# A planned attention and squared-ReLU kernel: the first batch's P.V split instead of zeroed, the first weights in two loads, and one Strassen block of tokens made plain again

## The chip, the cores and the metric

The kernel runs on one core of a Trainium2 chip. The metric is the device time of one execution in microseconds. Before the change the median of three runs is 288.12 us. The engines are TensorE (PE; its weight loads are shown apart as PEld), VectorE (DVE), ScalarE (ACT), GpSimd (POOL) and SyncE (SP).

## The reference

Eight batches of eight heads, 576 positions of head size 64. Attention within a window of 32 positions to each side, then a two-layer network with squared ReLU over all 4608 tokens:

```python
scores = q @ k^T / sqrt(64)                       # per batch and head, 576 x 576
scores = where(|i - j| <= 32, scores, -1e9)
attn = exp(scores - max) / (sum + 1e-9)
x = (attn @ v)  -> [4608 tokens, 512]             # heads side by side
h = x @ w_in                                      # 512 -> 2048
out = (max(h, 0) ** 2) @ w_out                    # 2048 -> 512, float32
```

## The kernel before

**Attention.** Each batch is three parts of 192 query positions, 24 parts in all, numbered G = 0 to 23. For a part, k and q are loaded as bf16 (`load_qk` on POOL's queue, L377; three of the first loads go through `load_hw` on SP and ACT as float32 into `ts` and are cast, L391 to L394). Parts below NTG = 9 are transposed on PE (`turn_pe`, L463) and copied to `kq` by ACT or DVE (L476, L477); the others by a transposing DMA (`turn_dma`, L491). `scores` multiplies keys by queries for two blocks of 128 keys (w = 0 and 1), eight heads each (L531), takes exp on ACT (L554), and multiplies by the 0/1 mask on DVE (L562): with MP = 1 both blocks in one instruction, unless the part is below NSPLIT = 6.

`pv` multiplies the probabilities by v with a column of ones (L590), twice into the same pair of banks: after the first (w = 0), rows 64 to 127 of the bank are finished; they are divided by their sums (L604, L608) into `xa`. After the second, all 128 rows are finished and divided into `xb`. Between them, rows 64 to 127 are set to zero (L614 on ACT or L615 on DVE), since the second product adds to what stands there. For parts below NZ there is no zeroing: the second product of each head is made in two column halves of its weights, and the half for rows 64 to 127 starts afresh:

```python
split = w and not full                     # full = G >= NZ
for z in range(0, 128, 64 if split else 128):
    n = 64 if split else 128
    mm = e.matmul(ps[z:z + n, c:c + 65], ptt[:, 4 * (h % 2) + h // 2, z:z + n], vt[:, w, h, 0:65],
                  start=((w == 0 or (z == 64 and split)) and y == 0), stop=True, skip_group_check=True)
```

`xturn` transposes x, on PE for parts below NXT = 9 (L630, L636, copied to `xt` by L644 or L646, called XT), later by DMA on SP.

**Network.** Tokens go through w_in in tiles of 192, 192, 192, 192 and 256, then 512. `mm1` (L690) is the plain form: 16 blocks of 128 hidden units, each four matmuls as wide as the tile, then ReLU (L664, L665) and square (L659, L660). For a tile in PAIR two blocks share a two-bank tile and one ReLU of 1024 columns. `mm1s` (L770) is the Strassen-Winograd form of a 512-token block: for each of four groups of hidden units seven products of four 256-column matmuls, with sums on DVE (L742, L794, L800) and seeds and copies on ACT (L809, L670). It is used for the blocks that MM1S lists. The second layer is plain for the first four tiles of 128 tokens (`mm2`, L835) and seven products for each later block (`strassen`, L917, with its sums on DVE, L859, L885, L949). A `wash` (L895) is one matmul of zeros over a bank, where the order's list of slots marks it with w.

Weights come on POOL's queue: w_in in four column quarters (`load_w1`, L431), w_out in four row quarters (`load_w2`, L436). With W1H a quarter of w_in comes in two loads.

**Order.** Every operation is recorded once, with its reads and writes. A text, ORDER, gives each recorded operation a letter for its engine (P, A, D, G for POOL, S for SP) and a start in nanoseconds; it is followed by the slot of each buffer. `apply` sorts each engine's instructions by these starts; nothing else is taken from them at run time, and semaphores hold the order between engines. Before 40 us `fill` puts small matmuls on zeros (L299) into the planned gaps of PE, at one for 56 ns, and ahead of the first transposes 39 plus one for every 56 ns beyond 3.9 us.

Of the kernel before, what the change touches and what calls it, by code (L numbers as in the profile page):

```python
# [21 lines left out]
    MM1S=(2048, 2560, 3072, 3584, 4096),  # L22
# [9 lines left out]
    PAIR=(1536,),  # L32
# [6 lines left out]
    W1H=(),  # L39
    TAIL=0,  # L40
    FP=1,
    MP=1,
    S34=1,
    NZ=0,
# [5 lines left out]
    NPT=4,  # L50
# [182 lines left out]
class Gen:  # L233
# [7 lines left out]
    def alloc(self):  # L241
# [733 lines left out]
    def record(self):  # L975
# [81 lines left out]
        at(4.0, self.sums_w2, 4.0)  # L1057
        if cfg["MM1S"]:
            at(4.5, self.sums_w1, 4.5)
# [30 lines left out]
P12475 D13910 D14180 D14966 P15634 D16146 D16416 P15114 P17172 A17612 P10615 D11167 P11225 A12456 P13361 A13996 D15461  # L1090
P13786 A15024 D18507 P16216 D17102 D17822 A18577 P19276 D19746 D20016 P19536 P20851 D21291 P15344 A16867 P14211 A16052
P17665 A19186 D21843 P20426 A21061 D24619 P22598 D23081 D23933 A25450 P26388 D27094 D27364 P24838 P28702 D30325 G20932
G21768 G20096 G16920 G24920 G29504 P41968 D42573 P40496 A41308 P43262 A43897 D45015 P18517 D22528 P43687 A45477 D46595
P19766 A23151 A24140 P45774 D46386 D47280 D48036 P49140 D49610 D49880 P51114 P51344 D51838 P21081 A23646 P23518 D25304
A27788 P26648 A28603 P27308 A29188 D29773 P29592 D34242 G23392 G22604 G27188 G27976 G43361 G45917 P45432 D48531 P47354
A47906 P28042 D34864 A35487 P49400 A50035 D51153 P24178 D25856 P51574 A52352 D53470 P25068 A26479 A29683 P52442 D53127
D54155 D54911 P55806 D56291 D57177 P57386 P58583 D59595 P21913 D23281 D33556 D38025 D37340 D38711 D35969 D45700 D43192
D57862 P22858 A24955 A26974 P25728 D30878 D26409 D32871 D28050 D36654 D28735 D40069 D31430 D32185 P30912 A32202 A32787
P30252 A31122 G26448 G28764 G24180 G25708 G46801 G48521 P47696 D49083 P47986 A49216 P28932 A31707 A36301 P50689 A51324
D52442 P31572 D35417 P51999 A53380 D55406 P44772 A47399 A57337 P55546 D56091 D56491 D58548 P59473 D60148 D60900 P58011  # L1100
P62644 D63084 P36348 D40754 P46034 A46904 A55037 P33960 D39396 P34620 P37008 P38736 P40891 A42229 A59141 P42363 A43233
D50565 P44112 A44982 G45081 G44245 G52653 G47685 G59793 G63781 P57616 A59521 P59733 A60443 P46694 A48721 D64189 P61994
A62994 A64112 D65507 P52702 A55852 P54886 A56842 A62179 P67289 D67759 D68029 A68941 P73039 D73509 D73969 P74079 P75183
A75994 P33096 P35484 P37872 P39632 A40706 A94765 P56066 A58646 P58813 D60348 A61364 P54226 A56347 P56726 A58152 D75340
P60992 D63636 G51029 G42573 G55017 G54229 G58121 G50145 P58241 D59043 P61652 D62204 P32232 P48276 P49825 P53362 A54436
S113850 P76293 A78955 A80051 P65775 A66795 A67913 D69031 P68422 A69549 P71033 D71620 D71890 D72645 P73299 D73769
D74655 P73849 P75413 D75893 P67549 A70240 D70934 P63738 D64821 P64611 A65695 D70249 P60128 P62874 P66425 P69295 A70842
A129316 P71293 A72376 G67125 G57381 G53489 G55805 G65453 G59005 P73559 A74059 P65485 D66725 P74309 A75393 D77130
G56545 G51817 G62945 G49309 G64665 G87303 P75643 A76809 A77927 D79045 S69616 S68326 P70159 A71443 P81919 D82389 D82659
A83760 P84769 D85318 D85588 P103901 P105644 D106314 P72166 A73249 D76445 P77816 A79450 D80263 D86274 D83345 D88177  # L1110
D84100 P85893 P86767 A87851 P89154 P94023 D99960 D95953 A104236 P90288 P91162 D92246 P97154 P98891 A99975 P94897
P102153 D104943 S139197 P101279 P103027 D106866 A116182 P105874 P106748 A107832 A121814 P79543 D80948 A81704 P82179
A85997 P85029 A86689 A95145 G61369 G66337 G60581 G62157 G79875 G75935 P81269 A82732 A84368 D86959 S67036 S71616 P76953
D78026 P90028 D93131 D93401 A94157 P96634 D99005 D99275 S94157 S100030 P83906 A85396 D88863 P80406 D81634 P83043
D89548 A96173 P78679 A80866 P98028 D101178 D101934 G77607 G68701 G69441 G78347 G86419 G104247 P87641 A88501 A89619
D90737 S83639 S91003 P92296 D96638 P92036 D92931 D94087 D95458 P96894 D97364 D97634 S102530 S101280 P95771 A97394
D98319 P88291 A90647 P93159 D94772 D105628 P99765 A103635 P104781 A107159 D108769 G75099 G80759 G84699 G67865 G76819
G100393 P100629 A101489 A102607 D103725 S95407 S92293 P115980 P117103 A118177 A122194 D102619 D116722 D111687 D117608
D112915 P114232 P115106 A116562 P118227 P119101 D120503 A120185 S128302 P121098 P124573 D125657 P122835 P126960
A130126 P127834 P128708 D132956 S140937 P133035 P135657 D136741 S137497 P133909 P134783 A135867 A145085 P108272  # L1120
D109455 D109725 A110480 P111985 D112455 D114133 S112600 S123182 P119975 P121972 D123292 D124580 P112505 P113369
A114442 D121921 G79087 G83911 G83123 G82335 G85535 G107255 P104131 A105013 A106131 D107551 S88423 S96697 P110259
P111122 A112195 A120786 P112245 D112715 D114819 A115574 P117967 D118437 D119322 S115574 S120642 P131309 P132172
A133245 A134363 P108532 P109395 D110469 D131165 G74359 G105775 G81595 G106515 G113703 G108975 P107622 A108839 A111088
D115504 S89713 S111310 P123709 P125447 D128729 D134746 P116843 D117408 D118637 D120008 P120838 D121721 D122606 S119392
S137947 P129582 P130445 A131519 D134060 D132536 D133641 D126840 D135431 P136531 A137178 P138055 D138702 A140576
P138492 D139388 P139820 A141177 P140517 D141869 P142702 D143772 A148131 D155834 P143399 A145465 A150362 P137618
A139974 P140954 A143077 D154996 P142265 A143678 P143836 A144483 P145147 D145794 P145584 D146691 D148062 D149699
P146718 A147530 A151565 P146281 A146928 P148029 A149159 A155866 P150651 D151298 P151348 A152167 P152222 D152939
P153096 D154310 D155415 A156467 P153970 A155264 A160153 P148466 A149761 P151785 A152768 A153460 P152659 D153625  # L1130
P153533 A154663 P155281 D156557 P158116 D159103 D162111 D164054 P159427 A160754 A161446 D128044 D131851 D135851
D140073 D137427 P138946 P141391 A142475 P144273 P147155 D148482 A150964 S154259 P148903 P149777 A154061 P154407
P155718 A158523 P157242 P158553 D159788 S160544 P159864 P161388 D163369 S164124 P162262 P163136 A164220 S190571
G109763 G110599 G90491 G108139 G111435 G134127 P126310 A127170 A128288 D129947 S124432 S125722 P140257 D140759 D141029
A141784 P143139 D144458 D144728 S146733 S145483 G116259 G117047 G117835 G99605 G133243 G140625 P136968 A137828 A138946
D142554 S130042 S128752 P146021 D146491 D147377 D150385 P151088 D151984 D152254 S150563 S153009 G112223 G112963
G105035 G103507 G160271 G141509 P156592 A157495 A159125 D160474 S127012 S121892 P164447 D164917 D165187 A166025
P167766 D168462 D169359 S165943 S185090 D158684 D161692 D162950 D162530 P164010 A164822 P165581 A166633 D180492
P166018 D167091 P167329 A167976 P168026 D168673 P168900 D170044 D172948 A175430 P169774 A170421 A173626 P164707
A165423 P166455 A168578 D176379 P166892 A169781 P169337 A172334 P170648 D173367 P174664 D175693 A177060 D182129  # L1140
P174227 A176458 D187961 P165144 A167234 P168463 A169179 A174829 P170211 A171023 P171085 A171732 P171782 D176798
P176849 D178169 D180073 A181534 P184751 A185398 A186601 P179684 A180331 P181869 A182562 A188976 P182566 A183213
# [80 lines left out]
```

## Time and profile before

| | |
|---|---|
| median of three runs | 288.12 us (288.11 to 289.0) |
| the profiled execution's own time | 288.54 us |
| its span, first to last instruction | 286.7 us |
| granted TensorE clock, mean | 1.000 |
| busy: PE, PEld, DVE, ACT, POOL | 280.1, 232.0, 236.0, 201.7, 117.9 us |
| mean DMA rate | 135 GB/s |

The span is shorter than the execution's own time by what lies around the first and last instruction. Busy times are sums of the instructions' spans; a matmul's span overlaps the next, so a busy TensorE is not one at its peak. In a row of the groups stand line, engine, operation, output and input, then busy time and the mean of one, then the idle time ahead of it and what ended it. In the chain of waits each row is a start, a length, and the work on the chain, the last column its number of instructions.

### The profile page before, as it was taken

How to read it: one execution, taken by the hardware profiler on the slowest of the kernel's cores; microseconds unless marked ns; L12 is line 12 of the kernel's file. 1: busy time of each engine (PE TensorE's matmuls, PEld its weight loads, DVE VectorE, ACT ScalarE, POOL GpSimd, SP SyncE). 2: the span in 40 equal slices, each digit the busy share in tenths (PEclk: the TensorE clock that was granted, in tenths of full speed). 3: DMA queues.
4: the chain of work that ended last, by engine and by line, in shares of the span. 5: the costliest groups of instructions: out<-in, count | busy, mean ns of one | idle time of the engine just before them, and what ended most of it. 6: DMA issues, size and time to landing. Idle time of an engine off the chain costs nothing.

```text
span 286.7 us, 7639 instructions
## 1 busy us (share of the span) xinstructions
PE 280.1 (98%) x3097; PEld 232.0 (81%) x3115; DVE 236.0 (82%) x424; ACT 201.7 (70%) x302; POOL 117.9 (41%) x153
## 2 busy tenths in 40 slices
PE   8999999999999999999999999999999999999995
PEld 8979858787857775776898898988888888888884
DVE  2779968878898988979889889899999989979631
ACT  1777638887795476636878899888887768776520
POOL 8999109998693269403702994310000000000000
PEclk9999999999999999999999999999999999999999
DMA  9999999999999999999999999998720431102123
GB/s 147 157 192 204 205 161 148 144 158 148 162 141 150 182 148 143 194 163 186 135 195 158 144 162 155 134 189 137 148 53 13 134 87 40 37 2 71 41 91 130
DMA packets 171107, 38.62 MB, mean 135 GB/s; under 512 B 158272, under 2 KB 170560, under 8 KB 171072
## 3 DMA queue, kind: packets, MB, share of 16 engines
q0 software_dynamic: 121920, 18.98, 94.4%
q1 hardware_dynamic: 43344, 14.30, 29.0%
q10 hardware_dynamic: 5808, 4.85, 5.5%
q8 instruction: 25, 0.41, 0.6%
q14 instruction: 10, 0.08, 0.1%
HBM read 38.80 MB, written 9.44 MB: 168 GB/s over the span
## 4 chain that ended last, share of the span: by engine, by line
PE 93%; DVE 3%; ACT 2%; issue 1%; ACTq 0%
PE ps L917 34%; PE ps L770 22%; PE ps L690 19%; PE ps L835 5%; PE ps L590 4%; PE ps L531 4%; PE ps L299 3%; PE ps L463 2%; ACT e L554 1%; PE ps L630 1%; DVE pt L562 1%; PE ps L636 1%; DVE xa L608 0%; ACT oe L670 0%; DVE xb L608 0%
## 5 line engine op out<-in xcount | busy, mean ns | idle before, releaser
L690 PE MATMUL ps<-xt,w 128*128 128x192 bf16 (+2 forms) x438 | 60.9, 286 | 0.7 <-issue 0.3
L670 ACT ACTIVATE oe<-ps 128x512 f32<-128x512 f32 x62 | 36.0, 596 | 29.4 <-PE ps L917 16.6
L554 ACT ACTIVATE e<-ps 128x1024 bf16<-128x1024 f32 x48 | 48.6, 1021 | 11.0 <-PE ps L531 8.9
L665 ACT ACTIVATE rt<-ps 128x512 bf16<-128x512 f32 (+2 forms) x76 | 44.0, 594 | 16.7 <-PE ps L690 9.6
L377 POOL DMA_DIRECT2D raw<-in_k_dram x46 | 36.4, 810 | 35.9 <-DMA kq<-raw 21.7
L690 PEld LDWEIGHTS ps<-xt,w 128*128 128x128 bf16 x448 | 38.7, 98 | 13.8 <-DVE xt L646 0.3
L377 POOL DMA_DIRECT2D raw<-in_q_dram x46 | 36.9, 815 | 27.3 <-DMA kq<-raw 26.5
L917 PE MATMUL ps<-w,gt 128*128 128x256 bf16 x384 | 47.3, 273 | 0.0
L659 ACT ACTIVATE gt<-rt 128x512 bf16<-128x512 bf16 (+2 forms) x56 | 43.2, 793 | 2.6 <-DVE rt L664 1.8
L415 POOL DMA_DIRECT2D v<-in_v_dram x48 | 42.0, 887 | 6.1 <-PE ps L590 6.1
L917 PEld LDWEIGHTS ps<-w,gt 128*128 128x128 bf16 x384 | 36.8, 98 | 6.0 <-issue 0.6
L562 DVE TENSOR_TENSOR pt<-e,mask 128x2048 bf16<-128x2048 bf16 (+1 forms) x30 | 30.3, 1009 | 3.9 <-ACT e L554 3.5
L770 PE MATMUL ps<-xs,sw 128*128 128x256 bf16 x240 | 32.7, 272 | 0.0
L917 PE MATMUL ps<-ts,gt 128*128 128x256 bf16 x256 | 31.7, 273 | 0.0
L917 PE MATMUL ps<-ts,ss 128*128 128x256 bf16 x256 | 31.4, 273 | 0.0
L794 DVE TENSOR_TENSOR rt<-ps,oe 128x512 bf16<-128x512 f32 x40 | 27.3, 687 | 4.0 <-PE ps L770 3.2
L917 PEld LDWEIGHTS ps<-ts,ss 128*128 128x128 bf16 x256 | 24.4, 98 | 3.7
L917 PEld LDWEIGHTS ps<-ts,gt 128*128 128x128 bf16 x256 | 24.7, 98 | 3.1
L770 PEld LDWEIGHTS ps<-xs,sw 128*128 128x128 bf16 x240 | 23.0, 98 | 2.6
L660 DVE TENSOR_TENSOR gt<-rt 128x1024 bf16<-128x1024 bf16 (+2 forms) x40 | 23.3, 590 | 0.5 <-ACT rt L665 0.4
L770 PE MATMUL ps<-xt,w 128*128 128x256 bf16 x160 | 22.1, 273 | 0.1
L664 DVE TENSOR_SCALAR rt<-ps 128x512 bf16<-128x512 f32 (+2 forms) x28 | 19.0, 685 | 2.1 <-PE ps L690 1.3
(69 smaller groups left out, 389.9 us busy)
## 6 DMA issues: line engine op xcount, KB each, us to landing
out_dram<-oe SPq DMA_DIRECT2D x19, 256.0 KB, 3.0
out_dram<-oe ACTq DMA_DIRECT2D x17, 256.0 KB, 2.5
v<-in_v_dram POOLq DMA_DIRECT2D x32, 128.0 KB, 5.7
w<-in_moe_w_in_dram POOLq DMA_DIRECT2D x4, 512.0 KB, 9.6
w<-in_moe_w_out_dram POOLq DMA_DIRECT2D x4, 512.0 KB, 16.7
raw<-in_q_dram POOLq DMA_DIRECT2D x18, 96.0 KB, 5.3
raw<-in_q_dram POOLq DMA_DIRECT2D x14, 112.0 KB, 4.9
raw<-in_k_dram POOLq DMA_DIRECT2D x14, 112.0 KB, 4.6
```

The costliest lines, as they stand in the source:

```text
L377: self.p.rec("POOL", lambda e, j=j, dst=dst: e.dma_start(dst, s[j]), writes=[self.rtag(t, b, g, j)], dma=(f"{t}{G % self.cfg['NRAW']}{j}", ...
L415: self.p.rec("POOL", lambda e, j=j, lo=lo, hi=hi, k0=k0: e.dma_start(vt[lo - k0:hi - k0, j, :, 0:64], self.v[b, :, lo:hi, :].rearrange("h ...
L554: last = self.p.rec("ACT", lambda e, ef=ef, v=v: e.activation(ef(), self.bank(v, 0, 2), ACTF.Exp, scale=0.125), reads=[v], writes=tags, ke ...
L562: self.p.rec("DVE", lambda e, pf=pf, ef=ef, mb=mb, n=n: e.tensor_tensor(pf(y=0, n=n), ef(y=0, n=n).rearrange("p (w h q) -> p w h q", w=n, ...
L659: alt = ("ACT", act(c), lambda e: e.activation(dst, src(), ACTF.Square)) if self.cfg["ALT"] else None
L660: self.p.rec("DVE", lambda e: e.tensor_tensor(dst, src(), src(), ALU.mult), reads=rd, writes=wr, key=key, dur=dve(c), name=name, alt=alt, ...
L665: return self.p.rec("ACT", lambda e: e.activation(dst(), src(), ACTF.Relu), reads=rd, writes=wr, key=key, dur=act(c), name=name, alt=alt, ...
L670: self.p.rec("ACT", lambda e: e.activation(dst(), src(), ACTF.Copy), reads=rd, writes=wr, key=key, dur=act(c), name=name, alt=alt, bias=se ...
L690: mm = e.matmul(ht[:, n * x:n * x + n], self.W1[:, ft, 128 * d:128 * d + 128], self.XT[:, ft, r:r + n], start=(ft == 0 and x == 0), stop=( ...
L770: mm = e.matmul(bk[:, 256 * x:256 * x + 256], lhs(k, 256 * m + 128 * x), rhs[:, k, :], start=start and x == 0 and k == 0, stop=(k == 1), s ...
L794: add.append(p.rec("DVE", lambda e: e.tensor_tensor(hs(), src(), self.oe(u), ALU.add), reads=[tg, u], writes=[(hh, y)], key=kk, dur=dve(51 ...
L917: mm = e.matmul(op[:, 256 * y:256 * y + 256], lhs[:, l0[0] + k, a:a + 128], rhs[:, r0 + k, c0:c0 + 256], start=start and y == 0 and k == 0 ...
```

## The change

It sets eight values of the configuration and replaces the written order.

- NZ from 0 to 3: in the three parts of the first batch the second P.V runs in column halves, and the zeroing of these parts goes.
- W1H from none to (0,): the first quarter of w_in comes in two loads of 256 columns.
- MM1S loses 2048: tokens 2048 to 2559 go through `mm1` in the plain form.
- PAIR loses 1536: that tile's ReLUs are 512 columns wide.
- MP from 1 to 0: in every part each block of 128 keys is masked by itself; NPT, the slots for masked probabilities, goes from 4 to 3.
- ORDER is another one, with other engines for some copies and other buffer slots. In it, among others: the copy of the first turned q is on DVE; ACT issues the loads of q's third part behind the first k copy; w_out's four loads stand behind the first k and q loads of the second batch; the turns of the second batch's first k and q stand ahead of most of the first MM1 blocks; one wash is marked where there were two.

```diff
 CFG = dict(
     NSTD=4,
-    MM1S=(2048, 2560, 3072, 3584, 4096),
+    MM1S=(2560, 3072, 3584, 4096),
...
-    PAIR=(1536,),
+    PAIR=(),
...
-    W1H=(),
+    W1H=(0,),
     TAIL=0,
     FP=1,
-    MP=1,
+    MP=0,
     S34=1,
-    NZ=0,
+    NZ=3,
     VC=99,
     PR=0,
     NV=5,
     NRAW=4,
     NE=2,
-    NPT=4,
+    NPT=3,
...
 ORDER = """
-D900 G1350 A129696 D1800 D9508 D10128 D10418 D10688 D7198 D9088 D12405 D8968 D7698 D8398 D9408 D7398 D2020 D9308 D7818
-D8108 D17412 D9928 D12805 D13710 D7498 D9708 D12605 D17302 D8683 D14866 D23833 D17702 D39949 S900 D4366 S1350 D6598
-G1700 G2488 G4852 G4064 G5640 G3276 G8840 G7216 A900 A13271 A1350 A6839 G6428 G9580 G7956 G10464 G11348 G12128 G14580
-G15360 G17756 G16140 G12908 G13792 G18536 G19316 P7268 A7873 P8308 A8860 P9765 A10400 D11719 P10190 A11428 D13025
...
+D900 G1350 A151905 D1800 D2310 D9258 D9698 D9968 D3570 D6996 D10278 D6876 D7216 D3285 D9478 D3770 D17192 D21022 D2020
+D16902 D2995 D8768 D9038 D10078 D2795 D12029 D18612 D19674 D2510 D22912 D43824 D9578 D33348 S1350 D6276 S900 D4366
+G1700 G2488 G4852 G4064 G3276 G5640 G9868 G10608 A8472 A13562 A8922 A15210 G6428 G7216 G8100 G8984 G12128 G11348
+G12908 G16140 G14572 G23360 G21792 G13688 G15352 G27244 G28764 P6946 A7551 P7664 D8216 P8838 A9473 D10591 P9263 A11316
...
```

More of the change, by code (lines that the diff above doesn't have):

```diff
@@ L1091 @@
[L1091 to L1135, printed above, removed]
@@ new lines @@
+A167431 P168355 A169002 A175667 P169666 A171079 P170103 A172282 P171851 D173107 P174296 D175364 D176119 D180725
+P178052 D180039 A193159 P167221 A168032 P169229 A169876 D170784 P168792 A170477 P170977 A171680 P171414 D172422
+P172985 D173993 D178179 D179284 P173422 A174464 D184955 P167918 D169413 P172288 A172935 A176877 P170540 A173863
+P173859 A175066 P174733 D176538 P176044 D177294 A179243 D182096 P177615 A178262 D190311 P180887 A181534 P182458
+A183105 A187147 P182895 A183706 P184206 A185336 P184643 D186530 P187088 D188320 D189206 A189695 P187525 A188350
@@ new lines @@
+A189041 D162089 D163660 D167772 D168528 D171204 P175170 P176481 A177565 P180013 P181324 D183737 A182408 S200812
+P178489 P185080 A186545 P183332 P185954 A187748 P187962 P188836 D190730 A192779 P190360 P191234 D194843 S195598
+P192108 P193632 A194870 A200401 G119201 G117481 G128061 G126485 G150268 G131309 P148989 A150877 D152776 A149849
+D152091 S142213 S139633 P157498 D157968 D158238 A158994 P160370 D161133 D161403 S160375 S173390 G120825 G148000
+G129781 G124957 G135380 G164434 P155974 A156834 D158924 A157862 D160028 S154845 S153555 P161504 D162774 D164345
@@ new lines @@
+A166721 P167658 D169213 D170099 S174640 S172140 G130569 G149528 G148788 G166058 G147116 G146328 P162638 A163498
+D165716 A164906 D166402 S157385 S170850 D186111 D187901 D193206 D191415 P194506 A195471 P196708 A197355 A202757
+P196271 A197956 P198716 D200178 P199590 D200933 P201338 D203793 D205849 A206338 P202212 A203960 A216204 P195834
+D196481 P198279 D199492 A203359 P199153 A199800 P200901 A201548 P201775 D202422 P203523 D204478 D210502 A217407
+P203960 D205163 D209127 P205968 A207366 P208153 A208800 A210700 P208850 A209497 P209724 A211301 P210598 D212862
@@ new lines @@
+P213220 D218459 D219832 D223949 P214354 A215001 D218040 P204657 A205304 P206405 A207968 A213157 P206842 D208442
+P209287 A210098 P210161 D210921 P211035 D211682 D213548 D214586 P213917 A215602 A216805 D187216 D201619 D191835
+D197852 D193625 P194960 P197145 A198558 P200027 P202649 D207224 A204562 A211903 P205094 P211472 A212556 P207279
+P212346 A213759 P214791 P215665 D217355 A229489 P217189 P218063 D219147 A220491 P218937 P219811 D220937 S221692
+P172725 D173793 D174678 A176269 P177355 D177979 D178598 S184131 S185381 G163598 G172458 G152680 G151844 G169210
@@ new lines @@
+G174082 P179363 A180271 D181410 A184308 D185426 S177180 S178521 P182198 D182781 D183051 A185937 P186828 D189006
+D189625 S186631 S196048 G151056 G171670 G169998 G168422 G170786 G166798 P189710 A190723 D192520 A191751 D195528
+S182391 S181101 P198019 D198537 D198807 A202149 P204397 D206268 D206538 S199562 S226954 D215957 D216446 D213967
+D216935 P224468 A226437 P227310 A228888 D240239 P228184 A230897 P231680 A232327 P234302 D237693 P234739 D238448
+A239204 D244228 P239546 D241753 A242508 P225779 D230419 P231243 A233957 D249250 P232117 D233580 P235176 A235823
```

117 lines of the change are left out of this document (67 added, 50 removed), and 12 rows, old and new, of the table ORDER.

## The prediction

> **What bounds the kernel now.** I read first the page's busy line, then the busy time in four stretches, then the chain of waits through the opening, and last the groups by form, the tiles and the waits for the prices.
>
> ```profile
> span 286.7 us, 7639 instructions
> PE 280.1 (98%) x3097; PEld 232.0 (81%) x3115; DVE 236.0 (82%) x424; ACT 201.7 (70%) x302; POOL 117.9 (41%) x153
> ...
> 0.00:20.00 20.00, 18.46 (x297) 17.04 (x298) 11.89 (x43) 11.94 (x15) 19.05 (x29) 1.00 1.63 164
> 20.00:40.00 20.00, 19.95 (x217) 16.32 (x215) 18.39 (x36) 11.60 (x19) 9.85 (x13) 1.00 1.51 195
> 40.00:130.00 90.00, 88.34 (x1007) 65.27 (x1019) 74.62 (x124) 63.05 (x87) 57.75 (x73) 1.00 1.92 157
> 130.00:283.50 153.50, 153.31 (x1585) 133.37 (x1586) 131.14 (x222) 114.51 (x182) 31.22 (x39) 1.00 0.88 109
> ...
> L299 PE MATMUL ps<-zz 128*128 128x128 bf16 x161 | 13.7, 251 | 1.2 <-DVE zz L293 1.2
> ...
> L299 PE MATMUL ps<-zz 128*128 128x128 bf16 x159 | 13.4, 251 | 1.2 <-DVE zz L293 1.2
> ```
>
> The columns of the four stretches are length, then busy time of PE, weight loads, DVE, ACT and POOL, then granted clock and DMA. The first L299 row is for the whole span, the second for its first 20 us. From 130 us on TensorE is busy 153.31 of 153.50 us, so in that half only TensorE work counts and a vector instruction more or less is hidden. From 40 to 130 us it is idle 90 - 88.34 = 1.66 us. The first 20 us look as busy, but 159 of the 161 idle matmuls (L299, on zeros, which fill planned gaps) run there: TensorE is waiting for the first batch. So the time is the opening, plus all TensorE work behind it, plus at least 1.66 us of later stalls. The change touches all three.
>
> **TensorE work.** The prices are spacings in the chain of waits (start, length, work; the last column counts matmuls).
>
> ```profile
> 113.02 1.73 PE ps L690 x8
> 246.79 8.73 PE ps L770 x80
> 55.83 0.51 PE ps L590 x16
> 43.34 0.62 PE ps L531 x16
> 29.35 3.30 PE ps L690 x40
> 37.42 3.45 PE ps L835 x16
> ...
> L895 PEld LDWEIGHTS ps<-zz 128*128 128x128 bf16 x2 | 0.2, 98 | 0.0
> ...
> PEld ps L531 <- issue: 2.8, 11, 0.4
> ```
>
> Tokens 2048 to 2559 in plain form are 16 blocks of 4 matmuls of 512 columns: 64 x 1.73/8 = 13.84 us. As seven products they are 4 x 7 x 4 = 112 matmuls of 256 columns: 112 x 8.73/80 = 12.22 us. That adds 1.62 us, in a stretch with nothing to hide it.
>
> Each split second P.V is 16 matmuls for 8, three times. The trace shows no column-half matmul. At the 0.51/16 = 0.032 us of a full-width one, 24 more cost 0.77 us. The nearest tiled form, the scores (L531, two halves of the rows), is the lower end: 0.62/16 = 0.039 us for 128 columns, against 0.216/4 = 0.054 us by the plain spacing, so halves partly overlap, and the whole of the 0.77 could go. The upper end adds a start-up on each side: weight loads of L531 stood 2.8 us in 11 waits with nothing to wait for, at most 0.4 each, so 0.77 + 3 x 2 x 0.4 = 3.2 us. I take 0.77, by the row of the same line; the bounds are 0 and 3.2.
>
> The Trainium skill (TensorEngine Tiling (Array Packing), Key Properties) says that changing the tiling mode drains TensorE while different tiles run in parallel. The 11 issue waits ahead of L531 agree with a drain; no run here shows column tiles. By the drain alone the sum would be higher, by parallel tiles alone lower, and my bounds from rows hold both.
>
> One of two 512-column washes (L895, the slots marked w) goes: -0.22 us. Leaving out the paired tile of tokens 1536 to 2047 keeps its 64 matmuls. TensorE work in sum: 1.62 + 0.77 - 0.22 = **+2.2 us** (bounds +1.4 to +4.6).
>
> **The opening.** The chain of waits from the first instruction:
>
> ```profile
> 1.19 6.89 PE ps L299 x71
> ...
> 8.47 0.56 PE ps L299 x10
> ...
> 9.38 1.01 PE ps L299 x18
> 10.38 0.55 PE ps L531 x16
> ...
> 15.06 0.49 DVE ps L615
> ...
> 18.88 0.61 ACT ps L614
> 19.49 0.18 issue
> ...
> 20.31 0.66 PE ps L690 x8
> ...
> 8.51 1.71 ACT L476 ACTIVATE kq<-ps 128x896 bf16<-128x896 bf16 x2 [0.80 <-PE ps L463]
> 18.60 0.83 PE L690 MATMUL ps<-xt,w 128*128 128x192 bf16 x8
> ...
> L431 POOL DMA_DIRECT2D w<-in_moe_w_in_dram x4: 780/795/816, 11.3 to 15.2; - x4
> ...
> ACT raw L393 <- DMA ts<-in_q_dram: 3.9, 1, 3.9
> ...
> DMA to landing us min/median/max: 3.9/4.8/5.9
> ...
> 4.00:7.00 3.00, 3.00 (x31) 3.00 (x29) 1.00 1.78 191
> 7.00:8.00 1.00, 1.00 (x19) 0.91 (x16) 1.00 2.41 153
> ```
>
> (a) Zeroing. Before the second P.V, rows 64 to 127 of the bank are zeroed. Two of the three stand on the chain: 0.49 us on DVE at 15.06, and 0.61 + 0.18 us on ACT at 18.88. Without them the second P.V starts right behind the division into xa (L608), which both forms must wait for. That is up to -1.3 us; the third zeroing is off the chain.
>
> (b) In the written order the copy of the first turned q moves from ACT to DVE. Before, ACT copies k and q one behind the other until 10.22 (8.51 + 1.71), and the first scores start at 10.38. In the written order the masks that DVE builds there come behind that copy, so the two copies can overlap: up to -0.8 us. The fill also shrinks: its formula gives 65 idle matmuls ahead of the first turn for 71, then 4 for 10 and 13 for 18, so it does not hold the scores back. The two last rows (idle matmuls alone) show 31 in 3 us and then 19 in one: TensorE went at half its pace until about 7 us, though the granted clock reads 1.00. Six fewer at 1/19 us end the fill 0.3 us earlier, still behind 7 us, so the turns run at the full pace; were they not to, 8 turns cost 0.4 us more.
>
> The Trainium skill (TensorE: Matmul & The Clock Gate, Part 1) puts the release of the slow clock at about 4 us of activity, run-variable. The pace here changes later, about 6 us after the first matmul; by either the first turns are at full pace, and the sum stays.
>
> (c) The load of q's third part moves on ACT's queue from 0.7 us to behind the first k copy, and the first of its two casts stands on ACT ahead of the second part's later exponential, the third part's k and q copies and XT0, the copy of the first transposed x. In the trace these loads (the row of tile ts, with k's first two) landed in 3.9 to 5.9 us, and one cast waited 3.9 us. I cost it at nothing; if it lands 1 us later than ACT gets to it, everything named waits 1 us.
>
> (d) The first weights come in two loads: one POOL issue more (0.8 us by L431). First use of w1 was at 18.60 behind XT0, so I cost it at nothing; and w2's four loads now stand behind the next batch's first k and q loads, which is a rival below.
>
> (a) + (b) = -2.1 us counts only if TensorE has real work to start with earlier. Its work behind 20.31 is 192-column blocks that need the same transposed x, now earlier, so I take the whole: **-2.1 us** (bounds 0 and -2.5).
>
> **Vector work and later stalls.**
>
> ```profile
> L562 DVE TENSOR_TENSOR pt<-e,mask 128x2048 bf16<-128x2048 bf16 x18 | 22.0, 1221 | 2.2 <-ACT e L554 2.1
> L562 DVE TENSOR_TENSOR pt<-e,mask 128x1024 bf16<-128x1024 bf16 x12 | 8.3, 691 | 1.7 <-ACT e L554 1.4
> ...
> 42.57 0.64 DVE kq L477
> ...
> 51.47 1.03 ACT e L554
> ...
> POOL raw L377 <- PE ps L463: 13.5, 2, 13.1
> ```
>
> Eighteen masks of 1221 ns become 36 of 691: 18 x (2 x 0.691 - 1.221) = 2.9 us more on DVE, most of it between 40 and 200 us, where DVE is 74.62/90 = 83% busy. DVE has 15 us free in that stretch, so it hides; if it did not, it would cost up to 2.9. In return the first half of P waits for one exponential and not for two. The plain tokens take away sums, seeds and copies, in a stretch where TensorE hardly ever waits: nothing. Two-bank relus become twice as many of half the size: hidden likewise.
>
> At 42.57 TensorE's chain runs through the copy of batch two's first turned k, 0.64 us plus 0.14 to the scores at 43.34, and POOL stands 13.1 us for that turn. The written order brings this turn ahead of most of the first MM1 blocks, so the stall goes: -0.5 us of the 0.78 (bounds 0 and -0.8). What is late next is the exponential at 51.47, 1.03 us, which I leave as it is.
>
> **Sum.** 2.2 - 2.1 - 0.5 = -0.4 us on a profiled run of 288.54 us (span 286.7), which is 0.4 above the median of 288.12. So 288.12 - 0.4 = **287.7 us**. About 0.3%, or 0.9 us, is what a measurement of this kernel can tell from no change; the forecast lies within.
>
> **Rivals.**
> Faster: the stalls of 40 to 130 us go too, since loads, turns and scores of the second batch run earlier, and POOL's 13.1 us pause with them. Then the 1.66 us shown idle fall by all but 0.5 (0.5 is counted above already): a further -0.7; and if the split halves overlap, -0.77. Together 287.7 - 1.4 = 286.3; either alone gives 287.0. For it: POOL's pause. Against: DVE's 83% and the added masks. Chance 0.33.
>
> Slower, by w2, with rows of tile w in the first 60 us and of the groups from 18 to 42.2 us:
>
> ```profile
> L436 POOL DMA_DIRECT2D w<-in_moe_w_out_dram x4: 819/840/856, 15.9 to 18.9; - x4
> DMA to landing us min/median/max: 6.6/13.0/19.4
> ...
> L835 PE MATMUL ps<-w,gt 128*128 128x512 bf16 x34 | 8.0, 379 | 0.1
> L690 PE MATMUL ps<-xt,w 128*128 128x192 bf16 x152 | 14.2, 246 | 0.0
> ```
>
> w2 was issued from 15.9 us on and landed within 19.4 us. Its user L835 ran 34 matmuls up to 42.2 us (a few records are missing), 34 x 3.45/16 = 7.3 us. If w2's later parts come some 8 us later, this filler is gone. In its place stands what is left of the first batch's three blocks of 64, 40 x 3.30/40 = 3.3 us, and about 1 us of the second batch's turns and scores: a hole of 3.0 us if nothing of w2 has landed by 42 us, half if two parts have. I take 2.3: 290.0. For it: DVE at 18.39 of 20 us in that stretch, so relus cannot free banks much quicker. Against: x of the third block and the second batch's scores come earlier too. Chance 0.13.
>
> Slower, by the opening: the 2.1 us do not arrive, because the late q load (c) or DVE, which now also has the q copy, ends last; then only +2.2 - 0.5 is left: 289.8. Chance 0.10.
>
> **How the numbers follow.** Forecast 0.44, faster 0.33, the two slower ones 0.23. With its parts between their rows (the split at 0 or at the start-up's first 0.4 x 3 on top) the forecast reaches from 286.9 to 288.9; on the fast side the range goes to 286.4, on the slow side to 289.9, which takes in the opening's case (289.8) and leaves out w2's at 290.0 and the far end of the faster one, about 2 in 10. With one of its two steps alone (287.0) the faster case still beats 0.3%, and both slower ones miss it on the other side: faster 0.33, same 0.44, slower 0.23.
>
> **What would show it.** Right: 16 matmuls of L590 with halves in the first three second P.Vs, spaced near 0.032 us; no zeroing ahead of them; first scores at 9.4 to 9.7 us; the first row of MM1 spaced as now but the last x of batch one earlier; POOL busy between 30 and 40 us; L690 up by 64 matmuls of 512 and L770 down by 112. Wrong: idle matmuls (L299) beyond 20 us in more than the 2 of now, a gap of L690 and L835 between 30 and 45 us, ACT waiting over 1 us for the second q load, or stalls in 40 to 130 us above 1.66.

## The result and the profile after

The changed kernel takes 292.46 us (median of three runs, 290.45 to 293.46) against 288.12 us, a ratio of 1.0136 [1.0114, 1.0158]. It is slower, where 287.7 us and 286.4 to 289.9 were forecast. The ratios, with their 95% intervals, are of runs in the faster of the two states that a kernel's runs show; one run of a0_after was in the slower one. The profiled execution took 292.46 us, 3.92 more than the one before.

The page's first lines of the changed kernel, for those of before:

```profile
span 290.6 us, 7526 instructions
...
PE 279.8 (96%) x3044; PEld 225.2 (77%) x3063; DVE 238.7 (82%) x443; ACT 189.9 (65%) x282; POOL 118.4 (41%) x154
```

The same four stretches (length, busy PE, PEld, DVE, ACT, POOL, granted clock, DMA share, GB/s):

```profile
0.00:20.00 20.00, 16.63 (x291) 15.04 (x292) 12.24 (x42) 10.45 (x13) 19.06 (x29) 1.00 1.52 151
20.00:40.00 20.00, 19.56 (x258) 17.97 (x259) 15.21 (x33) 10.18 (x17) 15.25 (x20) 1.00 1.74 184
40.00:130.00 90.00, 89.07 (x950) 61.82 (x961) 79.20 (x141) 61.95 (x87) 55.52 (x71) 1.00 1.89 159
130.00:283.50 153.50, 150.82 (x1519) 127.26 (x1524) 130.68 (x228) 106.72 (x166) 28.57 (x37) 1.00 0.89 110
```

TensorE's recorded busy time is the same, 279.8 us for 280.1; it now stands idle for 10.8 us of the span where it stood idle for 6.6. The two ends lost: 20 - 16.63 = 3.37 us idle in the first 20 us (before 1.54) and 153.5 - 150.82 = 2.68 us behind 130 us (before 0.19).

The idle time from 40 to 130 us, 1.66 us before and 0.93 after, is for the larger part no idle time. In both traces the records of some matmuls are missing, and each leaves a hole of 0.05 us or more. In the trace of before that stretch has 1019 weight loads and 1007 matmuls. The same order with lighter loads late in the kernel (e12 below, line numbers one higher) left a trace without such holes. Where before shows a hole and three matmuls, it shows four, and its idle time in that stretch is 90 - 89.42 = 0.58 us:

```profile
53.64 0.05 issue
53.70 0.81 PE ps L835 x3
...
53.33 0.86 PE ps L836 x4
...
40.00:130.00 90.00, 89.42 (x1021) 65.33 (x1020) 75.02 (x125) 63.31 (x87) 55.79 (x73) 1.00 1.70 147
```

The first two rows are of before, the last two of e12. Of the 2.68 us behind 130 us, 2.3 are waits: 1.3 for transposed x, 0.5 that ACT ended and 0.5 that DVE ended.

What TensorE waited for in the first 40 us, in the view of the waits (total, times, longest):

```profile
PE ps L463 <- DMA raw<-in_k_dram: 1.0, 1, 1.0
PE ps L590 <- DMA v<-in_v_dram: 0.7, 1, 0.7
PE ps L690 <- DMA w<-in_moe_w_in_dram: 0.4, 1, 0.4
```

None of the three stood there before; all are loads on POOL's queue. The chain of the first 30 us no longer runs through vector work but through one of these loads:

```profile
11.08 1.49 POOL w L431 x2
12.57 10.13 DMA w<-in_moe_w_in_dram
...
22.75 2.81 PE ps L690 x32
25.56 0.25 PE ps L590 x8
25.81 1.32 PE ps L690 x16
27.13 0.38 PE ps L590 x16
```

The later loss has its place in the chain too. The lines below, from the chain between 120 and 145 us, are the issue of a transposing load on SP's queue (L649), the flight of 8.10 us of the next one, a load of x issued at 128.13 (L652), and the plain block of tokens 2048 to 2559 that starts when it lands:

```profile
127.58 0.51 SPq L649
...
128.13 8.10 DMA xt<-xb
...
136.48 1.02 PE ps L690 x4
```

TensorE was ready for it at 135.2 us, 7.1 us behind its issue. Before the change the same load was issued at 121.09 and landed at 126.46. Its first reader was a sum on DVE for the Strassen form, 0.26 us later:

```profile
126.72 0.42 DVE L742 TENSOR_TENSOR xs<-xt 128x512 bf16<-128x512 bf16 x1
```

TensorE's first product of that form waits for all four of these sums and started at 136.9, 15.8 us behind the issue of the load. The transposing loads between 100 and 180 us took, from issue to landing, in the kernel before

```profile
DMA to landing us min/median/max: 2.5/5.6/8.5
```

and in the changed one

```profile
DMA to landing us min/median/max: 2.5/7.3/9.7
```

A flight of 8 us was thus nothing unusual before. TensorE was then 15.8 us away, with the short sums in between; 7.1 us do not cover it.

### The profile page after: what moved, and what is told of

It reads as the page before. It is cut to its first block, busy times and chain, and to the rows that moved or that the text cites. A ratio compares the mean times of both kernels' runs of the same rounds, so it can differ in the third digit from the quotient of the medians.

```text
span 290.6 us, 7526 instructions
## 1 busy us (share of the span) xinstructions
PE 279.8 (96%) x3044; PEld 225.2 (77%) x3063; DVE 238.7 (82%) x443; ACT 189.9 (65%) x282; POOL 118.4 (41%) x154
## 4 chain that ended last, share of the span: by engine, by line
PE 86%; DMA 6%; POOL 4%; issue 1%; DVE 1%; ACT 1%; SPq 0%; POOLq 0%; DVEq 0%; ACTq 0%
PE ps L917 32%; PE ps L690 22%; PE ps L770 17%; PE ps L835 5%; PE ps L590 4%; PE ps L531 4%; DMA w<-in_moe_w_in_dram 3%; DMA xt<-xb 3%; POOL raw L377 2%; PE ps L463 1%; POOL v L415 1%; PE ps L636 1%; POOL w L431 1%; PE ps L630 0%; DVE xa L608 0%
## 5 line engine op out<-in xcount | busy, mean ns | idle before, releaser
L690 PE MATMUL ps<-xt,w 128*128 128x192 bf16 (+2 forms) x499 | 75.0, 297 | 2.7 <-DMA xt<-xb 1.3
L665 ACT ACTIVATE rt<-ps 128x512 bf16<-128x512 f32 (+1 forms) x79 | 44.4, 576 | 26.9 <-PE ps L690 16.4
L690 PEld LDWEIGHTS ps<-xt,w 128*128 128x128 bf16 x512 | 44.2, 98 | 20.6 <-issue 1.7
L659 ACT ACTIVATE gt<-rt 128x1024 bf16<-128x1024 bf16 (+2 forms) x47 | 38.8, 841 | 4.4 <-DVE rt L664 2.9
L562 DVE TENSOR_TENSOR pt<-e,mask 128x1024 bf16<-128x1024 bf16 x48 | 32.7, 686 | 3.7 <-ACT e L554 3.2
L664 DVE TENSOR_SCALAR rt<-ps 128x512 bf16<-128x512 f32 (+1 forms) x41 | 25.5, 626 | 3.1 <-PE ps L690 2.4
L770 PE MATMUL ps<-xs,sw 128*128 128x256 bf16 x192 | 25.2, 273 | 0.0
L794 DVE TENSOR_TENSOR rt<-ps,oe 128x512 bf16<-128x512 f32 x32 | 21.5, 687 | 3.5 <-PE ps L770 3.1
L590 PEld LDWEIGHTS ps<-v,pt 128*128 128x128 bf16 (+1 forms) x408 | 17.6, 99 | 4.9 <-ACT e L554 0.8
L590 PE MATMUL ps<-v,pt 128*128 128x65 bf16 (+1 forms) x408 | 19.8, 194 | 1.1 <-DMA v<-in_v_dram 0.7
```

What stands on the lines that cost most here:

```text
L562: self.p.rec("DVE", lambda e, pf=pf, ef=ef, mb=mb, n=n: e.tensor_tensor(pf(y=0, n=n), ef(y=0, n=n).rearrange("p (w h q) -> p w h q", w=n, ...
L659: alt = ("ACT", act(c), lambda e: e.activation(dst, src(), ACTF.Square)) if self.cfg["ALT"] else None
L665: return self.p.rec("ACT", lambda e: e.activation(dst(), src(), ACTF.Relu), reads=rd, writes=wr, key=key, dur=act(c), name=name, alt=alt, ...
L690: mm = e.matmul(ht[:, n * x:n * x + n], self.W1[:, ft, 128 * d:128 * d + 128], self.XT[:, ft, r:r + n], start=(ft == 0 and x == 0), stop=( ...
L770: mm = e.matmul(bk[:, 256 * x:256 * x + 256], lhs(k, 256 * m + 128 * x), rhs[:, k, :], start=start and x == 0 and k == 0, stop=(k == 1), s ...
```

## The experiments

**The changed kernel again.**

> The changed kernel once more, as the base of the next three. Its first three times lay between 290.45 and 293.46 us, the kernel before between 288.11 and 289.0; all theories expect 290.4 to 293.5, median near 292, and a first wait on w_in near 22.7 us.

Measured: 291.92 us (291.62 to 297.42, 4 runs), 1.0126 [1.0111, 1.0141]. Its profiled run took 297.42 us, at a clock of 0.983 over the span. It shows one source of spread; the first three runs of this kernel, 290.45 to 293.46 us, had a clock of 0.999 or 1.000, so their spread has another. TensorE's part of the stretches (length, busy PE, granted clock, DMA share, GB/s):

```profile
14.00:18.00 4.00, 2.23 (x45) 0.88 1.75 178
18.00:22.00 4.00, 4.00 (x60) 0.50 1.46 197
22.00:24.00 2.00, 2.00 (x17) 0.53 1.50 196
24.00:26.00 2.00, 2.00 (x27) 1.00 1.51 197
184.00:188.00 4.00, 2.07 (x30) 0.97 2.08 152
188.00:190.00 2.00, 2.00 (x11) 0.50 1.20 280
190.00:192.00 2.00, 2.00 (x21) 0.72 1.22 258
```

Twice TensorE is busy for only 2.2 and 2.1 of 4 us, with waits for a DMA of 1.5 us (v) and 1.9 us (kq), and right behind it the granted clock is halved, once for 6 us and once for about 3. The share of clock lost, 1.7% of 295.6 us, is by estimate 5.0 us, about what lies between this run and the other profile (297.42 - 292.46). The Trainium skill (TensorE: Matmul & The Clock Gate, Part 1) says that the clock is gated to half when a window of some 3.4 us passes idle and released after as long a busy one. The halving agrees; it lasted about 3 us once and 6 us the other time, and the waits ahead of it, 1.5 and 1.9 us, were shorter than that window. Nor does every such stall do it: in the profiled run of e11_lateq_less TensorE waited 2.2 us for v at a granted clock of 1.00.

**The q load put back.** The loads of q's third part get the starts that they had before, ahead of ACT's other work.

```diff
-A8472 A13562 A8922 A15210
+A900 A13562 A1350 A15210
```

> The changed kernel with the two loads of q's third part issued by ACT at the start of its queue again (as in the kernel before), all else as in the change. Theory Q (these loads, at 7.6 us, take DMA time from POOL's queue, so that k's third part, v and the first weights land late and everything behind runs about 1.8 us late): the third k lands before 15 us instead of 16.8, TensorE's waits on loads between 15 and 23 us shrink from about 2 us to under 0.7, and the time falls by 1.3 to 2 us. Theory W (the first weights in two loads make them late): no change within 0.5 us. Theory N (the loss is TensorE's 2.2 us of added work and stalls after 130 us alone): no change within 0.5 us.

Measured: 291.13 us (290.12 to 293.95, 6 runs), 1.011 [1.0076, 1.0143]. TensorE's busy time in the first 20 us rises from 16.63 to 18.07 us, and none of the three waits above is left, so the opening's waits come from the late q loads. The time moved by only 0.8 to 1.3 us, inside the spread: the loss behind 130 us stayed (2.04 us idle there, 1.2 of it for the same `xt<-xb`).

**The first weights in one load**, with the q loads late, and (e3) with the q loads early.

```diff
-    W1H=(0,),
+    W1H=(),
```

> The changed kernel with the first quarter of w_in in one load again, at the start of the earlier half; one POOL issue (0.8 us) less. Theory W: the second quarter lands 1 us or more earlier than 22.7 us and the time falls by 0.8 to 1.8 us. Theory Q: the second quarter lands 0.5 us earlier at most, and the time falls by less than 0.5 us. Theory N: no change.

> Both of these undone. Q: as with the early q load alone, 1.3 to 2 us less than the changed kernel, near 290.4. W: as with one load alone. If each has a part, the sum of the two. N: no change. No theory expects it below 289.5, since the 2.2 us of added TensorE work stay.

Measured: 293.83 us (292.01 to 294.62, 5 runs), 1.0195 [1.0174, 1.0216], and 291.42 us (290.27 to 293.1, 6 runs), 1.0118 [1.009, 1.0145]. The second equals e1. The first lies above the changed kernel's interval, but three of its five runs had a clock of 0.992 to 0.994; the two at full clock, 292.01 and 292.68 us, lie among the changed kernel's. These spreads leave the question open; e13 and e14 below answer it.

**The q loads alone, on the kernel before.** Two more loads of the same size and queue at 8 us, into a buffer that nobody reads.

```diff
+            p.rec("ACT", lambda e, j=j, f=f, s=s: e.dma_start(f.rearrange("p (h d) -> p h d", h=8), s[j]),
+                  writes=[("t", 2, j)], dma=(f"x{j}", 0), key=0.0, dur=450, name=f"xq{j}")
...
+A7900 A7950
```

> The kernel before with two extra loads on ACT's queue at about 8 us, the same bytes as the two loads of q's third part, into a buffer that is free then; nothing reads them. Theory Q (a load on ACT's queue at that time takes DMA time from POOL's queue): the first quarter of w_in lands 1 to 1.5 us later than 17.9 us, v and k loads issued from 7 us on likewise, first MM1 0.3 to 1.3 us later than 18.6, time 288.4 to 289.5 and more spread between runs. Rival (POOL's queue is bound by its own issue, not by shared DMA time): landings and time as before, 288.1.

Measured: 290.03 us (289.61 to 291.15, 6 runs), 1.006 [1.004, 1.008]. Two loads that no one waits for cost 1.8 us against 288.22 us for the kernel before in the same series, more than theory Q put on them. Three of the six runs had a clock of 0.993 or 0.994; the other three, at full clock, took 289.61 to 289.81, so 1.4 to 1.6 us come without a loss of clock. The waits of its first 40 us:

```profile
PE ps L463 <- DMA raw<-in_k_dram: 1.8, 1, 1.8
```

The third k, on POOL's queue, landed at 16.69 us; before at 14.18. The first quarter of w_in landed at 20.51; before at 17.90. The stall again took the clock down behind it, to 0.63 from 18 to 20 us and then to half (columns as in the first table of stretches):

```profile
20.00:22.00 2.00, 2.00 (x20) 1.77 (x15) 0.98 (x2) 1.75 (x3) 2.00 (x4) 0.52 1.83 179
```

How the two queues share the DMA engines is seen in what each moved from 6 to 23 us (packets, MB, share). In the kernel before:

```profile
q0 software_dynamic: 13044, 2.95, 189.3%
...
q10 hardware_dynamic: 26, 0.01, 0.3%
```

and with the two loads added:

```profile
q0 software_dynamic: 12603, 2.62, 176.8%
...
q10 hardware_dynamic: 1624, 0.41, 13.7%
```

The first is POOL's queue, the second ACT's. 0.40 MB more on ACT's went with 0.33 MB less on POOL's, and POOL's loads are what TensorE waits for at that time. In the changed kernel ACT's queue moved 0.39 MB and POOL's 2.43, but there POOL's own order is another one too. The Trainium skill (DMA: Bandwidth & Descriptors, Queues, rings and completion order) says that a DMA engine takes packets from its queues in turn; these rows agree with that, though another way of sharing would give them as well.

**The zeroing alone, on the kernel before.** The three zeroing instructions go, the second P.V runs in halves, all else stays.

```diff
-    NZ=0,
+    NZ=3,
...
-D14966 A18577 A25450
```

> The kernel before with the split second P.V in the first three parts and without their three zeroings, all else in the written order of before. The prediction's terms: 24 matmuls more, +0.77 us at 0.032 each, bounds 0 to 3.2, and up to -1.3 us of zeroing off the opening's chain: 287.6. If the split drains TensorE at each change (rival): gaps of 0.2 us or more around each split P.V and 288.1 to 289. If nothing of the opening reaches the end: 288.1 to 288.9.

Measured: 288.38 us (288.03 to 288.79, 12 runs), 1.0002 [0.9992, 1.0012]: nothing. Its chain shows what took the place of the last zeroing of the two on the chain:

```profile
18.05 0.69 DVE xa L608
...
18.77 0.70 DVE pt L562
...
19.52 0.45 PE ps L590 x16
```

The second P.V now waits for the mask that DVE had behind the division, and starts at 19.52 us where it started at 19.67. That mask stood there before, too:

```profile
18.88 0.69 DVE L562 TENSOR_TENSOR pt<-e,mask 128x1024 bf16<-128x1024 bf16 x1
```

It ended at 19.57 us, so without the zeroing no more than 0.1 us could be won. The zeroing at 15.06 gave as little: DVE's next mask came at 15.08 us for 15.59, but the P.V stands on TensorE behind a turn of k or q and started at 15.71 us in both, and the division behind it at 16.45 for 16.55.

**The later x taken off the path.** e1, with the plain block of 2048 reading columns of w_in in place of the transposed x (so its result is another one).

```diff
-self.XT[:, ft, r:r + n],
+(self.W1[:, ft, 512:512 + n] if t0 == 2048 else self.XT[:, ft, r:r + n]),
...
```

> The changed kernel with the early q loads, and the plain block of tokens 2048 to 2559 streams columns of w_in in place of transposed x, so that it waits for no transposing DMA; its values are not the reference's there. Theory D (what is left of the loss is that x of these tokens is transposed by DMAs that land 8 us after issue, when POOL's loads fill the DMA engines, and the plain block stands on TensorE just ahead of their landing): the 1.2 us stall at about 134.5 us goes and the time falls by 1 to 1.6 us against the early q loads alone (median 291.1). Rival (the stall is made up later, or another transposing DMA ends last at the same place): less than 0.5 us.

Measured: 293.09 us (289.16 to 297.31, 6 runs). Four of the six runs had a clock of 0.987 to 0.994; the two at full clock took 289.16 and 290.29 us, where e1's five at full clock took 290.12 to 291.50. That points to a gain, as theory D has it, but two runs do not settle it. That other loads end late as well, so that taking away one use does not cure the loss, was not tested here.

**The masks alone, on the kernel before**: each paired mask as two instructions.

> The kernel before with the paired mask multiplication done by two instructions one behind the other, both behind the second exponential: the added DVE time of the unpaired form (18 x 0.16 = 2.9 us) without its earlier start. Prediction's term: hidden, 288.1 within 0.3. Rival (DVE is short between 40 and 130 us): up to 2.9 us more, and idle TensorE there above 1.66 us.

Measured: 288.38 us (288.22 to 289.17, 12 runs), 1.0001 [0.999, 1.0012]. They are hidden.

**Lighter loads for the later batches.** From batch index 5 on, the loads of q, k and v carry two of eight heads; everything else is done as before. e9 is e1 with that, e11 the changed kernel with that, e12 the kernel before with that.

```diff
-            self.p.rec("POOL", lambda e, j=j, dst=dst: e.dma_start(dst, s[j]),
+            nh = 2 if b >= 5 else 8
+            self.p.rec("POOL", lambda e, j=j, dst=dst, nh=nh: e.dma_start(dst[:, 0:nh, :], s[j][:, 0:nh, :]),
...
```

> The changed kernel with the early q loads, and from the sixth batch on each load of q, k and v carries only two of the eight heads (the other heads compute on what the buffers held, so the output is not the reference's for these batches). As many instructions on every engine, a quarter of the load bytes behind about 105 us. Theory D (what is left of the loss are transposing DMAs that land late because the DMA engines are full): no TensorE wait on a DMA behind 105 us, time 287.5 to 288.8, and runs within 1 us of each other instead of 4. Rival N (the loss is TensorE's added work and stalls on ACT and DVE): 290 or more.

> The changed kernel as it is (late q loads) with the lighter loads from the sixth batch on. Theory Q: 1.3 to 2.5 us above the same with early q loads, all of it lost before 25 us. Rival (the later loads decide, the opening is made up): within 0.5 us of it.

> The kernel before with the lighter loads from the sixth batch on, as the control. Theory D: its TensorE hardly waits for a DMA behind 105 us, so the time stays at 288.1 within 0.4. If it falls by 0.5 us or more, lighter loads alone speed any kernel and the step with the changed kernel says less.

Measured: e9 288.42 us (288.27 to 288.56, 11 runs), 1.0008 [0.9999, 1.0016]; e11 289.92 us (289.05 to 290.27, 6 runs), 1.0052 [1.0035, 1.0069]; e12 288.12 us (287.93 to 288.6, 11 runs), 1.0 [0.9992, 1.0009]. The kernel before gains nothing from lighter loads; the changed one gains 2.0 to 2.5 us and much of its spread goes. So it is the changed order that made the bytes of the later loads count. The transposing loads between 100 and 180 us now fly, in e9,

```profile
DMA to landing us min/median/max: 2.4/3.3/6.3
```

The stretches of e9:

```profile
0.00:20.00 20.00, 17.49 (x303) 15.69 (x304) 13.02 (x43) 11.70 (x14) 19.05 (x29) 1.00 1.66 165
20.00:40.00 20.00, 20.00 (x256) 17.80 (x254) 16.08 (x35) 10.49 (x18) 16.67 (x22) 1.00 1.72 185
40.00:130.00 90.00, 90.00 (x972) 62.75 (x971) 78.74 (x139) 62.09 (x87) 56.03 (x76) 1.00 1.73 151
130.00:283.50 153.50, 153.04 (x1542) 128.64 (x1540) 130.44 (x228) 105.42 (x166) 18.87 (x29) 1.00 0.46 87
```

and of e11, where all that differs is the late q load:

```profile
0.00:20.00 20.00, 15.95 (x285) 14.71 (x285) 11.63 (x41) 9.77 (x12) 19.05 (x29) 1.00 1.53 154
20.00:40.00 20.00, 19.85 (x268) 18.29 (x263) 15.81 (x35) 10.77 (x17) 15.28 (x20) 1.00 1.75 184
40.00:130.00 90.00, 90.00 (x963) 61.95 (x961) 78.91 (x140) 61.98 (x87) 57.63 (x78) 1.00 1.73 151
130.00:283.50 153.50, 153.50 (x1548) 129.34 (x1547) 131.64 (x230) 106.71 (x166) 18.92 (x29) 1.00 0.47 87
```

Behind 40 us no wait of TensorE is left in either; the 0.46 us of e9 lie behind its last matmul. The late q load costs 289.92 - 288.42 = 1.5 us, and e11's first 20 us hold 17.49 - 15.95 = 1.54 us less TensorE time than e9's.

**Less work in the plain block**: e9 without 8 of its 64 matmuls of 512 columns.

```diff
-                    for ft in range(4):
+                    for ft in range(3 if t0 == 2048 and d % 2 else 4):
...
```

> The same with fewer loads, and in the plain block of tokens 2048 to 2559 every second of the 16 blocks leaves out the last quarter of its sum: 8 matmuls of 512 columns less, 8 x 0.216 = 1.73 us, about what the plain form costs beyond the seven products. If TensorE's work there is on the path: 1.5 to 1.8 us below the kernel with fewer loads alone. If something else ends last there: less than 0.8.

Measured: 286.73 us (286.51 to 286.98, 5 runs), 0.9946 [0.9931, 0.9962]. That is 1.69 us below e9, for 8 x 0.216 = 1.73 of work: once the waits are gone, each matmul of that block counts at its full price.

**The weights' two loads, settled**: e11 and e9 with one load.

> The kernel of e11_lateq_less (late q loads, lighter loads of the later batches) with the first weights in one load. What is open is the price of the two loads, which e2_w1one and e3_both gave with too wide a spread. Theory A, the two loads are what lets the first network matmul start on half a quarter, and with the late q loads on the queue the single load lands later still: 290.7 to 291.5 us, 0.8 to 1.5 above e11's 289.92. Theory B, the two loads cost POOL one issue of 0.8 us and bring nothing: 289.0 to 289.9. Read on: the first 192-column matmul of L690, 20.2 us or so with two loads, and the work just before it on the chain.

> The kernel of e9_less (early q loads, lighter loads of the later batches) with the first weights in one load. Theory A, as for e13: slower than e9's 288.42, to 288.9 or above. Theory B: 288.42 less up to 0.8, so 287.6 to 288.4. Theory C, with the q loads early the weights land before their use either way, and the vector work of the second part ends last: 288.3 to 288.5, no difference.

Measured: 289.84 us (288.77 to 292.65, 12 runs), 1.007 [1.004, 1.0099], and 288.41 us (288.05 to 288.74, 12 runs), 1.0 [0.9987, 1.0013]. Neither can be told from its partner (289.92 and 288.42): theory C beside the early q loads, theory B at most beside the late ones. The two loads are worth nothing here. Four of e13's twelve runs had a clock of 0.988 to 0.994 and took 290.59 to 292.65 us, as three of e2_w1one's five had a low clock; why it falls in some runs and not in others stays open.

## Why the prediction was wrong

The steps from 288.12 us to the changed kernel:

| kernel | us | step |
|---|---|---|
| before | 288.12 | |
| the change, q load early, later loads light (e9) | 288.42 | +0.3 |
| the same with the q load late (e11) | 289.92 | +1.5 |
| the changed kernel, full loads | 291.92 and 292.46 | +2.0 to 2.5 |

The forecast's own sum, -0.4 us, is a sum for e9, which came out at +0.3. That the two lie this close is luck: the opening brought less than forecast and the work cost less, as the terms below show. The rest, 3.5 to 4.0 us, comes by way of transfers: one cause the prediction costed at nothing, the other not at all.

**The step that failed first is (c)**, the moved q load "at nothing". It asked who waits for this load, and rightly found that ACT would hardly: both casts ran on time, at 13.20 and 14.68 us, so the sign that the prediction named for it (ACT waiting over 1 us) does not show. What it did not ask is whose loads are in flight beside it. 0.39 MB on ACT's queue, in the middle of the first loads of k, v and w_in, delayed these on POOL's queue, and TensorE waited for k, v and w_in in turn. Issued early, this load has a price too: POOL's first q landed at 7.50 us in e1 and at 5.57 in the changed kernel, and the first scores came at 9.23 and 8.89. What that gained was lost again at the wait for v. e4 shows the effect on the kernel before (+1.8 us), e11 less e9 on the changed one (+1.5). The rival "slower, by the opening" named the late q load and put 289.8 us on it; its place was right, its mechanism (this load itself ends last) was not.

**The second step that failed is one that is missing**: the margin from the issue of each transposing load to its use. The prediction called the plain block work "in a stretch with nothing to hide it" and did not look at what feeds it. The new order leaves 7.1 us for a load that took 8.10. That the 2.0 to 2.5 us hang on the bytes of the later loads is shown by e9, e11 and e12, and the waits of 2.3 us behind 130 us are about as much; that this one load is the first of them is seen in the chain. How the sum splits over the several late loads, and what part is clock lost behind stalls, was not separated.

**Term by term**, with the balance of idle time. Its base is e12, which keeps the order of before and its time, and whose trace has no holes, like those of e9 and e11. Idle matmuls count 0.056 us each; e12 has 161 of them, e9 and e11 134. In e12's first 20 us TensorE is busy for 18.39 us.

| us against e12 | e11 | e9 |
|---|---|---|
| idle, 0 to 20 us | +2.44 | +0.90 |
| idle, 20 to 40 us | +0.15 | 0 |
| idle, 40 to 130 us | -0.58 | -0.58 |
| 27 idle matmuls fewer | -1.51 | -1.51 |
| profiled run less 288.05 | +1.89 | +0.22 |
| what that leaves for work | +1.4 | +1.4 |

- **Work, +2.2.** Right in kind: e10 shows that the plain block's work counts in full. By the balance some 1.4 us came; which part of the work was cheaper than forecast is not shown. The split came near its 0.77, but not by its reason. In the changed kernel's chain `27.13 0.38 PE ps L590 x16` against `25.56 0.25 PE ps L590 x8` is 0.13 us, and the first eight matmuls behind the split take longer as well, `27.51 0.77 PE ps L690 x8` against `41.59 0.66 PE ps L690 x8`: 0.24 us together. The starts in the trace say where it lies. Two halves start 2 to 5 ns apart, and the eight pairs take 0.25 us where eight whole matmuls take 0.22. From the last matmul of MM1 to the first half there are 0.176 us, ahead of a whole one 0.083; behind the last half 0.126, behind a whole one 0.033. So the 24 extra matmuls cost next to nothing and each change of form about 0.09 us: a start-up on each side, the mechanism of the upper bound, and halves that overlap, that of the lower one. That is 0.13 us where the first change falls into a wait and up to 0.24 elsewhere, 0.4 to 0.7 us for the three.
- **Opening, -2.1.** Even with the loads on time (e9) only 0.90 - 1.51 = -0.6 came. The scores did start earlier, at 8.89 us in the changed kernel and 9.34 in e9 (9.4 to 9.7 foretold, 10.38 before). But of the -1.3 of the zeroing about 0.1 came, as e5 shows: "right behind the division" was wrong, since the mask behind the division, and a turn ahead of the other P.V, ended almost as late. And the prediction took over the gain whole on the ground that the 192-column blocks need "the same transposed x, now earlier". They do not follow from it alone: e9's chain runs through DVE's masks and divisions of the first two parts, until the last turn and the first long run of MM1:

```profile
14.88 0.69 DVE xb L609
...
15.84 0.70 DVE pt L563
...
16.57 0.69 DVE xa L609
...
18.30 0.70 DVE xb L609
...
19.05 0.40 PE ps L637 x4
19.45 4.62 PE ps L691 x56
```

(Line numbers in e9 are one higher than in the changed kernel from the edited load on.) DVE ends last there, the other half of that rival's condition. In the written order MM1 stands behind the second part's last turn; before, eight of its matmuls ran ahead of it, at 18.60 us.

- **Stalls, -0.5 at 42 us.** The sum is about right, the place is not. All 0.58 us of e12 are gone in e9 and e11. But ahead of the scores at 43.34 us TensorE was idle for only 0.15 us, since it ran eight matmuls of MM1 from 42.37 on while DVE copied k; 0.42 us lay at 52 us, where the exponential ended last, which the prediction left as it is. The 1.66 us that it read as idle are mostly missing records (e8, with full loads, has 0.59), so the faster rival's further -0.7 had nothing to come from. POOL works on between 20 and 40 us (15.25 us busy for 9.85), as foretold.
- **Masks and the two loads of w_in, at nothing.** Right, by e8, e13 and e14.
- **w2 late.** Did not happen: the last idle matmul starts at 19.8 us, and L835 follows L690 without a wait.

## What to carry to other kernels

A transfer has two prices: who waits for it, and whose transfers it slows; where a moved load has slack of its own, look at what else is in flight at that time and who waits for that. For work that is put earlier or in another form, compare the time from issue to use of each load that feeds it with the longest flight of such loads in the trace, not with the median. A gain at the head of a chain arrives only as far as the next instruction on the engine that it releases is ready; when one step goes, name the one behind it in the same engine's order. And before small idle times of TensorE are priced, compare the numbers of matmuls and of weight loads in that stretch: a missing record looks like a stall.

## What the hardware showed that was not expected

- A wait of 1.5 to 2 us for a DMA can halve TensorE's granted clock for the next 2 to 6 us (0.50 to 0.53 in a0_after, 0.52 in e4_extra), so such a wait can cost more than its length; in the profiled run of e11_lateq_less one of 2.2 us did not. Over whole runs the clock lay below 0.997 in 19 of the 51 runs of a0_after, e1 to e4, e6, e11 and e13, the kernels with a load added or left late or with full later loads in the new order, and in none of the 63 runs of e5, e8, e9, e10, e12 and e14.
- Two loads of 192 KB that nobody waits for, beside a full queue, cost 1.8 us, 1.4 to 1.6 of it without any loss of clock.
- Matmuls on the two column halves of the weights start 2 to 5 ns apart, and eight such pairs take 0.25 us for the 0.22 of eight whole ones; the change to them and the change back cost about 0.09 us each.
